# Order of the first transfers: the second chunk's gates ahead of the first part of the input weight

## The chip, the cores and the metric

The kernel runs on one core of a Trainium2 chip. The metric is device time in microseconds of one execution, lower is better. Five engines work side by side, each through its own instructions in the order in which they were written: TensorE (PE, with its weight loads as PEld), VectorE (DVE), ScalarE (ACT), GpSimd (POOL) and SyncE (SP), which here issues nearly all transfers. An instruction that waits holds up everything behind it on its engine.

## The reference

Two layers follow each other. The first is a gated linear attention over batch 4, 8 heads, 768 steps, head size 48; the second a gated feed-forward of width 384 to 1024 to 384.

```python
f = 1 / (1 + exp(-f_logit))
for t in range(S):
    state = f[:, :, t, :, None] * state + k[:, :, t] x v[:, :, t]    # outer product per head
    y[:, :, t] = q[:, :, t] @ state
x = heads of y side by side                                          # [4, 768, 384]
h = relu(x @ w_in)                                                   # w_in  [384, 1024], float64
conv = conv_w[0] * h[t-1] + conv_w[1] * h[t] + conv_w[2] * h[t+1]    # conv_w [3, 1024], float64
out = (h * sigmoid(conv)) @ w_out                                    # w_out [1024, 384], float64
```

q, k, v and f_logit are float32; the weights arrive as float64 and are made single precision on the chip.

## The kernel before, in words

**Tiling.** Time is cut into 24 chunks of 128 steps (6 for each of 4 batches, `steps`, line 106). Within a chunk the recurrence is done by matrix products: the gates' logarithms are summed over time, their exponentials scale q and k, a masked score matrix `pa`/`am` gives the part inside the chunk, a state `st` carries the rest. The result `xT` (split in a high and a low half) feeds the hidden products `ph` with w_in, then come relu, the convolution and the gate in `g`, and the output products `po` with w_out.

**Order.** All work is written as small generators, one per stage and chunk or per weight part. `ORDER` (lines 26 to 79), a string written out by hand, names at each place the generator that makes its next step: `for e in ORDER.split(): next(todo[e], None)` (line 573). The schedule is manual, so each engine gets its instructions in just this order. `F0`, `F1`, ... load the gates of chunk 0, 1, ...; `x` is exp and ln of the gates on ACT (two steps); `G` their sum over time on PE for the first six chunks; `p` the two exponentials `fi` and `fd` on ACT; `L`, `M`, `V` load k, q and v; `K` and `Q` scale k and q on DVE; `a` the scores. `I0.0` loads rows 0 to 127 and columns 0 to 511 of w_in, and the steps `J0.0` make it single precision; `c` loads and turns conv_w.

**The loads.** `load_f` and `load_w_in` each issue one transfer on SP:

```python
def load_w_in(kt, i):                                                     # line 214
    nc.sync.dma_start(raw_in(kt, i), w_in[kt * P:(kt + 1) * P, i * WC:(i + 1) * WC].bitcast(I32))
def load_f(n):                                                            # line 255
    w = FW if n < PN else NP * P
    nc.sync.dma_start(fbs[n // GC][:, n % GC]...[:, :w], chunk(f_in, *steps[n])[:, :w])
```

A gates' transfer of the first six chunks has 128 rows of 400 float32 (200 KB), the weight part 128 rows of 512 float64 (512 KB). The buffers of both are allocated before the first transfer and are not shared.

**What follows on the loads.** The first steps on ACT are, in this order, exp and ln of chunk 0 (lines 268, 271), exp of chunk 1 (268), `fi` of chunk 0 (305), ln of chunk 1 (271), `fd` of chunk 0 (307), then the third step of `J0.0` (183). `fi` and `fd` of chunk 0 read `pl`, the sum over time of chunk 0's gates (sixteen matmuls, line 292). DVE scales k of chunk 0 by `fi` (line 317) and then q by `fd` (line 324). Making a weight single (`single`, lines 173 to 189) takes six steps over three engines:

```python
nc.gpsimd.tensor_scalar(mf, hf, F64_TOP, -F64_TOP, ALU.min, ALU.max)                  # 179
nc.gpsimd.tensor_scalar(sf, mf, 0.0, 1.0, ALU.mult, ALU.mult)                          # 181
nc.scalar.activation(mf, mf, AF.Copy, scale=2.0 ** -112)                               # 183
nc.scalar.activation(lw, lw.bitcast(U32), AF.Copy, scale=2.0 ** -29)                   # 185
nc.vector.scalar_tensor_tensor(m, m, 3, s, ALU.logical_shift_left, ALU.bitwise_or)     # 187
nc.vector.tensor_tensor(w.bitcast(I32), m, lw, ALU.add)                                # 189
```

Its tiles are named `mswi` and `wi` for w_in, `mswo` and `wo` for w_out, `mscw` and `c` for conv_w. Line 386 brings the state to the next chunk on POOL (`st`), and line 398 makes the products `py`, the last of which read `st`.

Of the kernel before, what the change touches and what calls it, by code (L numbers as in the profile page):

```python
# [23 lines left out]
TS = 24  # L24
ON_POOL = ""
ORDER = """
F0 I0.0 F1 x0 x0 c L0 M0 G0 x1 I1.0 F2 J0.0 p0 x1 p0 G1 J0.0 J0.0 c J0.0 K0 p1 L1 Q0 L2 J0.0 M1 x2 c F3 V0 a0 k0 J0.0
I2.0 c p1 x2 G2 H0.0 K1 c a0 x3 J1.0 J1.0 t0 Q1 I2.1 a1 y0 J1.0 k0 y0 J1.0 c V1 H0.0 J1.0 F7 c c J1.0 x3 a1 G3 J2.0 M2
M4 p2 J2.0 p2 H1.0 F4 y0 F5 J2.0 K2 s0 J2.1 y0 J2.0 x7 J2.0 y1 J2.1 t1 s0 p3 c L3 x7 t2 Q2 k1 k1 J2.0 I0.1 x4 G7 L4 J0.1
x5 V2 M3 K3 x4 y1 H1.0 J0.1 k2 a2 k2 a2 h0.2 x5 I1.1 O3 s1 y1 s1 F6 p3 J2.1 s1 J2.1 J2.1 H2.0 y1 Q3 J0.1 G4 J2.1 J1.1 G5  # L30
# [697 lines left out]
```

## Time and profile before

| what | us |
|---|---|
| three runs | 307.47, 304.69, 305.09 |
| their median | 305.09 |
| the profiled execution, its own time | 305.0 |
| its span from first to last instruction | 303.3 |

The profiled execution thus has 1.7 us around its span, and lies 0.09 us under the median. Times in the rows count from the span's start. A row of the timeline gives the start, the duration, engine, line, operation, tiles (out<-in), shape and count, and in brackets how long the engine sat idle before and what ended it. SP's rows are the issuing of transfers, not the moving of their data.

### The profile page before, as it was taken

What the parts mean: (1) busy time and instruction counts of PE and PEld (TensorE: products, weight loads), DVE (VectorE), ACT (ScalarE), POOL (GpSimd) and SP (SyncE); (2) the same over time, 40 slices, a digit from 0 to 9 for tenths busy, and PEclk for the clock granted to TensorE, in tenths of its full rate; (3) what the DMA queues carried; (4) which work ended last, traced back from release to release, by engine and by line L of the source; (5) the groups of instructions that cost most, each with busy time, mean ns of one, the idle gap of its engine ahead of it and who ended that gap; (6) DMA issues with size and microseconds to landing.
All of it is one profiled execution on the core that took longest, in us unless ns stands there. A gap on an engine that the chain in (4) does not pass through costs nothing.

```text
span 303.3 us, 8894 instructions
## 1 busy us (share of the span) xinstructions
PE 294.2 (97%) x3747; PEld 273.5 (90%) x3747; DVE 251.3 (83%) x380; ACT 220.5 (73%) x422; POOL 85.3 (28%) x107
## 2 busy tenths in 40 slices
PE   7799989999999999999999999999999999999994
PEld 5678878988999999999998999999999999999994
DVE  4999999999999999977999999946893976479520
ACT  4999979989967996767976995665756544676521
POOL 5475894344503140300323410230305010000000
PEclk9999999999999999999999999999999999999999
DMA  7999951194025411627315130602012000000211
GB/s 230 396 385 391 403 191 39 56 333 135 2 72 161 101 59 61 220 72 224 102 37 166 64 124 2 195 2 84 3 30 89 2 28 26 28 1 2 79 54 55
DMA packets 19374, 35.67 MB, mean 118 GB/s; under 512 B 2156, under 2 KB 9092, under 8 KB 19332
## 3 DMA queue, kind: packets, MB, share of 16 engines
q1 hardware_dynamic: 19044, 34.69, 33.8%
q8 instruction: 30, 0.49, 0.7%
q10 hardware_dynamic: 288, 0.39, 0.4%
q14 instruction: 12, 0.10, 0.1%
HBM read 30.35 MB, written 4.72 MB: 116 GB/s over the span
## 4 chain that ended last, share of the span: by engine, by line
PE 75%; DVE 7%; POOL 3%; issue 1%; ACT 1%; POOLq 0%
PE po L507 31%; PE ph L454 28%; PE py L398 8%; PE pa L351 3%; PE ptk L330 2%; DVE g L466 2%; PE pk L376 2%; DVE g L464 2%; DVE g L475 1%; POOL st L386 1%; PE pa L345 1%; DVE am L358 1%; PE pk L371 1%; POOL q L324 1%; DVE gl L495 1%
## 5 line engine op out<-in xcount | busy, mean ns | idle before, releaser
L454 PE MATMUL ph<-xT,wih 128*128 128x384 f32 x384 | 99.6, 340 | 0.0
L454 PEld LDWEIGHTS ph<-xT,wih 128*128 128x128 f32 x384 | 68.3, 188 | 1.0 <-issue 0.2
L507 PE MATMUL po<-woh,gh 128*128 128x384 f32 x192 | 64.7, 337 | 0.0
L454 PE MATMUL ph<-xT,wil 128*128 128x384 f32 x192 | 64.3, 335 | 0.0
L507 PE MATMUL po<-wol,gh 128*128 128x384 f32 x192 | 64.2, 334 | 0.0
L507 PE MATMUL po<-woh,gl 128*128 128x384 f32 x192 | 64.2, 334 | 0.0
L464 DVE SCALAR_TENSOR_TENSOR g<-hb,cw,g 128x384 f32<-128x384 f32 (+1 forms) x64 | 42.2, 667 | 13.0 <-ACT g L462 12.9
L466 DVE SCALAR_TENSOR_TENSOR g<-hb,cw,g 128x384 f32<-128x384 f32 (+1 forms) x64 | 40.5, 649 | 0.7
L457 ACT ACTIVATE hb<-ph 128x384 f32<-128x384 f32 x64 | 30.7, 487 | 11.4 <-PE ph L454 10.8
L495 DVE TENSOR_TENSOR gl<-g,gh 128x1024 fp32r<-128x1024 f32 (+4 forms) x34 | 30.4, 908 | 9.6 <-ACT gh L493 9.6
L462 ACT ACTIVATE g<-hb,cw 128x384 f32<-128x384 f32 (+1 forms) x64 | 38.0, 614 | 0.3
L507 PEld LDWEIGHTS po<-woh,gh 128*128 128x128 f32 x192 | 36.0, 188 | 0.5 <-issue 0.2
L324 POOL TENSOR_TENSOR q<-q,fd 128x512 f32<-128x512 f32 x19 | 26.9, 1419 | 33.0 <-ACT fd L307 24.3
L507 PEld LDWEIGHTS po<-wol,gh 128*128 128x128 f32 x192 | 36.0, 188 | 0.0
L507 PEld LDWEIGHTS po<-woh,gl 128*128 128x128 f32 x192 | 36.0, 188 | 0.0
L454 PEld LDWEIGHTS ph<-xT,wil 128*128 128x128 f32 x192 | 36.0, 188 | 0.0
L493 ACT CAST gh<-g 128x1024 fp32r<-128x1024 f32 (+4 forms) x34 | 26.4, 800 | 12.7 <-PE po L507 8.8
L386 POOL TENSOR_TENSOR st<-st,ft_all 128x256 f32<-128x256 f32 x16 | 20.8, 1301 | 51.7 <-DVE st L384 51.7
L475 DVE SCALAR_TENSOR_TENSOR g<-g,hb 128x768 f32<-128x768 f32 (+1 forms) x32 | 30.1, 952 | 3.7 <-ACT g L473 3.7
L512 ACT COPY ob<-po 128x384 f32<-128x384 f32 x24 | 11.3, 474 | 29.7 <-PE po L507 27.1
L473 ACT ACTIVATE g<-g 128x768 f32<-128x768 f32 (+1 forms) x32 | 26.7, 846 | 3.9 <-DVE g L466 3.8
L312 POOL COPY ft_all<-fd 128x4 f32<-128x4 f32 x24 | 12.7, 537 | 56.5 <-ACT fd L307 56.5
(92 smaller groups left out, 453.9 us busy)
## 6 DMA issues: line engine op xcount, KB each, us to landing
k<-in_k_dram SPq DMA_DIRECT2D x24, 256.0 KB, 4.4
q<-in_q_dram SPq DMA_DIRECT2D x24, 256.0 KB, 4.3
v<-in_v_dram SPq DMA_DIRECT2D x24, 224.0 KB, 4.3
fb<-in_f_logit_dram SPq DMA_DIRECT2D x18, 256.0 KB, 4.3
out_dram<-ob SPq DMA_DIRECT2D x22, 192.0 KB, 1.9
wis<-in_moe_w_in_dram SPq DMA_DIRECT2D x6, 512.0 KB, 6.0
wos<-in_moe_w_out_dram SPq DMA_DIRECT2D x8, 384.0 KB, 5.6
fb<-in_f_logit_dram SPq DMA_DIRECT2D x6, 200.0 KB, 4.9
```

Of the source, the lines that this page charges most:

```text
L324: (nc.vector if n < QV else nc.gpsimd).tensor_tensor(raw["q", n], raw["q", n], fds[n][1], ALU.mult)
L398: nc.tensor.matmul(py[G * p:G * p + G, t, :], lhs, rhs, start=start, stop=stop)
L454: nc.tensor.matmul(ph, w, xts[b, hf][:, t, xl, :], start=(k == 0), stop=(k == 3 * KT - 1))
L457: nc.scalar.activation(hb[:, 2:HS + 2], ph, AF.Relu, scale=0.5)
L462: nc.scalar.activation(cv, hb[:, 1:n + 1], AF.Copy, scale=cw[:, 1, f:f + 1])
L464: nc.vector.scalar_tensor_tensor(cv, hb[:, 2:n + 2], cw[:, 2, f:f + 1], cv, ALU.mult, ALU.add)
L466: nc.vector.scalar_tensor_tensor(cv, hb[:, 0:n], cw[:, 0, f:f + 1], cv, ALU.mult, ALU.add)
L473: nc.scalar.activation(cv, cv, AF.Tanh)
L475: nc.vector.scalar_tensor_tensor(cv, cv, 1.0, h_b[:, fp:fp + 2, 1:n + 1], ALU.add, ALU.mult)
L493: nc.scalar.copy(hi, g[:, f:f + k])
L495: nc.vector.tensor_tensor(lo, g[:, f:f + k], hi.bitcast(F32), ALU.subtract)
L507: nc.tensor.matmul(po, g[:, f, :], w, start=(i == 0), stop=(i == 3 * NF - 1))
```

## The change

Two neighbouring words of `ORDER`, the second and the third, change places. SP issues the gates of chunk 1 second and the first part of w_in third; every other transfer keeps its place, and no engine other than SP gets its instructions in another order.

```diff
 ORDER = """
-F0 I0.0 F1 x0 x0 c L0 M0 G0 x1 I1.0 F2 J0.0 p0 x1 p0 G1 J0.0 J0.0 c J0.0 K0 p1 L1 Q0 L2 J0.0 M1 x2 c F3 V0 a0 k0 J0.0
+F0 F1 I0.0 x0 x0 c L0 M0 G0 x1 I1.0 F2 J0.0 p0 x1 p0 G1 J0.0 J0.0 c J0.0 K0 p1 L1 Q0 L2 J0.0 M1 x2 c F3 V0 a0 k0 J0.0
 I2.0 c p1 x2 G2 H0.0 K1 c a0 x3 J1.0 J1.0 t0 Q1 I2.1 a1 y0 J1.0 k0 y0 J1.0 c V1 H0.0 J1.0 F7 c c J1.0 x3 a1 G3 J2.0 M2
```

## Rows read from the trace of the kernel before

**Rows 1.** The page: busy shares, then granted clock and DMA share in 40 slices.

```profile
PE 294.2 (97%) x3747; PEld 273.5 (90%) x3747; DVE 251.3 (83%) x380; ACT 220.5 (73%) x422; POOL 85.3 (28%) x107
...
PEclk9999999999999999999999999999999999999999
DMA  7999951194025411627315130602012000000211
```

**Rows 2.** The chain that ended last, in order of time: start, us, what.

```profile
39.11 4.25 POOL st L386
...
43.41 0.80 PE py L398 x24
```

**Rows 3.** Timeline of DVE, three stretches between 7 and 40 us.

```profile
7.60 0.69 DVE L317 TENSOR_TENSOR k<-k,fi 128x512 f32<-128x512 f32 x1 [2.17 <-ACT fi L305]
8.51 0.69 DVE L324 TENSOR_TENSOR q<-q,fd 128x512 f32<-128x512 f32 x1 [0.22 <-ACT fd L307]
...
35.95 1.03 DVE L195 TENSOR_TENSOR wil<-wi,wih 128x512 fp32r<-128x512 f32 x1
...
39.13 0.54 DVE L187 SCALAR_TENSOR_TENSOR mswo<-mswo 128x384 int32<-128x384 int32 x1
```

**Rows 4.** Waits of DVE from 8 to 46 us: who waited for what, us in total, times, longest.

```profile
DVE k L317 <- ACT fi L305: 2.2, 1, 2.2
DVE q L324 <- ACT fd L307: 0.2, 1, 0.2
```

**Rows 5.** Timeline of SP, the first 7 us.

```profile
1.36 0.42 SPq L215 DMA_DIRECT2D wis<-in_moe_w_in_dram  x1
1.82 0.43 SPq L259 DMA_DIRECT2D fb<-in_f_logit_dram  x1
...
4.60 1.48 SPq L276 DMA_DIRECT2D k<-in_k_dram  x2
```

**Rows 6.** Timeline of ACT from 3 to 13 us.

```profile
3.43 0.54 ACT L268 ACTIVATE fb<-fb 128x400 f32<-128x400 f32 x1 [1.26 <-DMA fb<-in_f_logit_dram]
4.00 0.54 ACT L271 ACTIVATE fb<-fb 128x400 f32<-128x400 f32 x1
6.48 0.54 ACT L268 ACTIVATE fb<-fb 128x400 f32<-128x400 f32 x1 [1.95 <-DMA fb<-in_f_logit_dram]
6.97 0.60 ACT L305 ACTIVATE fi<-pl 128x512 f32<-128x512 f32 x1
...
8.36 0.63 ACT L183 ACTIVATE mswi<-mswi 128x512 f32<-128x512 f32 x1
...
9.93 0.53 ACT L268 ACTIVATE fb<-fb 128x400 f32<-128x400 f32 x1
10.36 0.29 ACT L183 ACTIVATE mscw<-mscw 24x128 f32<-24x128 f32 x1
```

**Rows 7.** Timeline of POOL, three stretches between 5 and 44 us.

```profile
5.82 0.65 POOL L179 TENSOR_SCALAR mswi<-wis 128x512 f32<-128x512 f32 x1 [2.61 <-DMA wis<-in_moe_w_in_dram]
6.56 0.62 POOL L181 TENSOR_SCALAR mswi<-mswi 128x512 f32<-128x512 f32 x1
7.26 0.28 POOL L179 TENSOR_SCALAR mscw<-cws 24x128 f32<-24x128 f32 x1
7.63 0.82 POOL L181 TENSOR_SCALAR mscw<-mscw 24x128 f32<-24x128 f32 x1
...
35.55 0.88 POOL L179 TENSOR_SCALAR mswo<-wos 128x384 f32<-128x384 f32 x1
...
39.08 4.27 POOL L386 TENSOR_TENSOR st<-st,ft_all 128x256 f32<-128x256 f32 x1
```

**Rows 8.** Waits of SP from 0 to 40 us: who waited for what, us, times, longest.

```profile
SPq L276 <- DMA wis<-in_moe_w_in_dram: 0.7, 2, 0.5
```

**Rows 9.** Timeline of PE from 4 to 9 us.

```profile
4.95 1.98 PE L292 MATMUL pl<-tri,fb 128*64 128x128 f32 x16
```

**Rows 10.** Waits of PE over the whole span, one of five.

```profile
PE py L398 <- POOL st L386: 1.1, 1, 1.1
```

## Prediction

> **What bounds the kernel now.** I read the page first. PE is busy in 97% of the span, at the full granted clock in every slice; DMA is full in slices 1 to 5, that is from about 2 to 40 us, and far from full after that [rows 1]. So there is a head of some 43 us, in which inputs and weights arrive and are prepared, and then a long stretch that PE fills. Whatever changes in the order of the first transfers can only act through the head. Next I read the chain that ended last: it enters the PE stretch at 43.41, released by POOL's state product of 39.11 to 43.36 [rows 2]. To see what sets 43.4 us, I read the waits of DVE: from 8 to 46 us it has only two, one of 2.2 us that ends at 7.60 and one of 0.2 us that ends at 8.51 [rows 3, 4]. From then on DVE works without a pause until the end of the head, so a shift of DVE at 9 us is still there at 43, and from there goes into PE and the end. Last I read the timelines of SP, ACT, POOL and PE for the first 11 us, to see who stands before DVE's two waits.
>
> **The issues.** SP issued the weight at 1.36 and the gates of chunk 1 at 1.82, each for about 0.43 us, none waiting [rows 5]. They change places: gates at 1.36, weight at about 1.80. Nothing is added. They land one behind the other: POOL, which waits for the weight, starts at 5.82, and ACT, which waits for the gates, at 6.48, 0.66 later [rows 6, 7]. With the bytes ahead unchanged, the later of the two should land when the later one landed before: the weight at about 6.4. For the gates I take 3.43 (ACT's start on chunk 0's gates [rows 6]) plus 0.66, so 4.1; at worst 200/512 of the 2.39 us that the weight took from 3.43 to 5.82, so 4.4. The transfers behind (conv_w, k, q, the next weight) see the same sum of bytes ahead. One thing does move on SP: of the two k's issued from 4.60, the stretch is 1.48 us in place of twice some 0.43 [rows 5], so the second waited, and the waits of SP put that to the landing of a weight, 0.5 us at the longest [rows 8]. Now the gates hold that place and land first, and this k is issued up to 0.5 us sooner; it queues behind DMAs that are full anyway, so I count nothing.
>
> **What goes: ACT's wait of 1.95 us before exp of chunk 1.** ACT is free from 4.54 (4.00 + 0.54), so exp can run from then, two microseconds sooner. But behind it stands `fi` of chunk 0, which reads `pl`, and PE works on `pl` until 4.95 + 1.98 = 6.93 [rows 9]. `fi` starts at 6.97, 0.49 after exp; elsewhere ACT starts the next instruction 0.43 after the same exp (9.93 to 10.36) [rows 6]. So `fi` was waiting for PE already, and the wait that goes is replaced by another one that ends at the same time. Ends: nothing, or at most 0.06 (0.49 less 0.43). I take 0. The ln of chunk 1 stands behind `fi` and stays too.
>
> **What comes later: the weight, by about 0.64 us** (POOL's start at 5.82 becomes 6.46, about where ACT's start at 6.48 was). POOL's first step then runs 6.46 to 7.11, and the second, which followed at a distance of 0.74, from 7.20 to 7.82 [rows 7]. ACT wants it at 8.36 [rows 6]: 0.5 us of cover are left. Conv_w's two steps on POOL, which ended at 8.45, come some 0.6 later and are wanted on ACT at 10.36: covered too. For data alone the cost is nothing. It would cost only if the weight landed more than 1.18 us later than before (8.36 less 7.18, the end of POOL's second step).
>
> **What collides: POOL with DVE.** The second step moves from 6.56 to 7.18, when DVE was idle, to 7.20 to 7.82, and at 7.60 DVE starts on k of chunk 0 [rows 3, 7]. Such pairs hold each other up in this trace. Conv_w's second step, 24 rows of 128, took 0.82 where its first took 0.28: it began at 7.63, under DVE's k product, and ended 0.16 after that one (8.29). In the other direction, POOL's step at 35.55 stretched DVE's product at 35.95 to 1.03, where products of the same width take 0.69 [rows 3, 7]. So DVE's k product waits for POOL until 7.82 (0.22 late), ending at 8.51; just there q starts, which had an idle 0.22 in front. This swallows it: cost 0.0 to 0.1. Then conv_w's two steps (0.28 each) meet k and q instead of one of them meeting k alone; each can hold DVE once, at most 0.28, and DVE has no idle time left behind q. Upper end: 0.22 + 0.28 + 0.28 less the 0.22 idle, 0.56. Lower end: 0, if POOL does all the waiting, for it has 0.5 us and more to give. There is no row of this very pattern; the nearest is 35.55, where POOL slipped in once and cost DVE 0.34. I take a third of the upper end, 0.2, as one of the two conv_w steps finds DVE free at some point.
>
> The Trainium skill, page "SBUF — State Buffer", section "Who interferes with whom", says that a VectorE instruction with two SBUF inputs and a GpSimd instruction that reads SBUF exclude each other, and that the one that starts second blocks until the first is done. By it the k product at 7.60 loses to POOL's step and the q product loses nothing as long as conv_w's steps start behind it, which would make the sum 0.0 to 0.1 in place of 0.2. The trace agrees at 7.63 and 35.55; at 39.08 it doesn't, for there POOL started 0.05 before DVE and still took 4.27 us [rows 3, 7].
>
> **The sum.** 0.0 from ACT, 0.0 from SP and the DMAs, +0.2 from POOL against DVE, carried by DVE to 43 us and by PE to the end: 305.0 + 0.2 = 305.2 us against the profiled execution, 0.1 above the median of 305.09. That is far under 1% (3 us), about what a measurement of this kernel can tell from no change; the runs shown differ by 2.8 us among themselves.
>
> **Rivals.**
>
> (a) Faster, the wait was worth its length: 1.95 us off ACT and the end, 303.05. For it: it is ACT's longest wait in the stretch shown, and ACT's instructions stand close behind it [rows 6]. Against: `fi` can't start before `pl` is done at 6.93, and DVE waits for `fi`.
>
> (b) Faster, a race near the end of the head turns. POOL's state product took 4.27 us at 39.08, since DVE began a long run of products at 39.13 [rows 3, 7]; PE waited 1.1 us for it [rows 10]. If the shift lets POOL in first, PE gains up to this 1.1: 305.2 - 1.1 = 304.1. Against: what stands before both there follows DVE, so both are shifted alike and the distance of 0.05 stays.
>
> (c) Slower: the weight lands so late that POOL's second step starts under DVE's k product and has to wait for its end. The place is 7.6 us; it decides from a landing some 0.4 us later than I take (second step starting at 7.60 in place of 7.20). POOL then starts it at 8.29 and ends at 8.91, ACT's step of 8.36 waits until 8.95, 0.59 late, and POOL holds q on DVE from 8.51 to 8.91, 0.40 late. Both engines go on without a pause: 305.0 + 0.6 = 305.6. For it: the weight is the largest of the early transfers. Against: the sum of bytes ahead.
>
> (d) The swap does nothing at all, as the gates land together with the weight: 305.0.
>
> **How the numbers follow.** The forecast has 0.75: its own range is 304.9 (all gained, nothing paid: 305.0 less 0.06) to 305.6 (305.0 + 0.56). (a) has 0.04, since the row of `pl` speaks plainly against it; (b) 0.07; (c) 0.11; (d) 0.03. The range goes down to (b)'s 304.1, rounded to 304.0, and up beyond (c) to 306.5: a run of the kernel before has stood 2.4 us above its median, and a race as in (b) lost elsewhere would cost about the same 1.1 (305.2 + 1.1 = 306.3). None of the cases reaches 1% in either direction (302.0 or 308.1). The chances of that are what the scatter of runs and races that I don't see leave: 0.02 faster, 0.03 slower, 0.95 within 1%.
>
> **What would show it.** Right: ACT's exp of chunk 1 starts between 4.5 and 5 with no wait for a DMA; `fi` still starts at 6.9 to 7.0, now after a wait of about 2 us for PE; POOL's first wait, for the weight, ends near 6.45, about 0.65 later; ACT's step of line 183 still starts at 8.3 to 8.5; DVE's k product takes 0.8 to 1.0 in place of 0.69; the state product of POOL near 39 still takes about 4 us, and PE enters its stretch at 43.3 to 44.0. Wrong: `fi` starting well before 6.9 (rival a), a state product under 1.5 us near 39 (b), line 183 waiting for POOL (c), gates landing after 5.5 (d), or a change of more than 1 us that none of these rows accounts for.

## The result and the profile after

| | before | after |
|---|---|---|
| median of 16 runs each, us | 304.96 | 307.26 |
| lowest and highest | 304.03, 308.26 | 305.72, 308.29 |
| profiled execution, its span | 305.0, 303.3 | 306.96, 305.2 |

The ratio is 1.0064 with an interval of [1.0040, 1.0089]: slower, by 0.64% or about 2 us. That is under the 1% that I had named, but it is real, and it lies outside the range given (304.0 to 306.5). The two profiled executions differ by 1.96 us and their spans by 1.9, so they show a loss of that size.

The page of after, granted clock and DMA share in 40 slices, as in [rows 1]:

```profile
PEclk9789999999999999999999999999999999999999
DMA  6999981185023422527305230602003000000211
```

Two things are new. The granted clock is below full in the second and third slice, and the DMAs move a little less at the start and more later. The timeline of after, PE, ACT, DVE and POOL from 4.7 us, answers to [rows 3, 6, 7, 9]:

```profile
4.76 0.52 ACT L268 ACTIVATE fb<-fb 128x400 f32<-128x400 f32 x1
...
5.00 1.09 PE L292 MATMUL pl<-tri,fb 128*64 128x128 f32 x16 [0.29 <-ACT fb L271]
...
6.13 0.60 ACT L305 ACTIVATE fi<-pl 128x512 f32<-128x512 f32 x1 [0.85 <-PE pl L292]
...
7.34 0.68 POOL L179 TENSOR_SCALAR mswi<-wis 128x512 f32<-128x512 f32 x1 [4.14 <-DMA wis<-in_moe_w_in_dram]
...
8.06 0.69 DVE L317 TENSOR_TENSOR k<-k,fi 128x512 f32<-128x512 f32 x1 [2.63 <-DMA k<-in_k_dram]
8.10 1.13 POOL L181 TENSOR_SCALAR mswi<-mswi 128x512 f32<-128x512 f32 x1
...
8.68 1.08 DVE L324 TENSOR_TENSOR q<-q,fd 128x512 f32<-128x512 f32 x1
9.26 0.63 ACT L183 ACTIVATE mswi<-mswi 128x512 f32<-128x512 f32 x1 [1.62 <-POOL mswi L181]
...
9.82 1.16 PE L345 MATMUL pa<-q,k 48*128 48x128 f32 x16 [1.52 <-DVE q L324]
...
11.36 0.69 DVE L317 TENSOR_TENSOR k<-k,fi 128x512 f32<-128x512 f32 x1
```

Read from the top. Exp of chunk 1 starts at 4.76 without a wait, as the swap wanted. `fi` then waits for PE, and goes at 6.13, even earlier than the 6.97 of before, since PE's sum `pl` took 1.09 here and 1.98 there [rows 9]. But POOL gets the weight at 7.34, where it had it at 5.82 [rows 7], and DVE, which had waited for `fi` until 7.60 [rows 3], now waits until 8.06 for k of chunk 0 itself. POOL's second step starts 0.04 behind it and shares the stretch with both products of DVE: 1.13 for POOL, 1.08 for q in place of 0.69. ACT's step of line 183 waits 1.62 for POOL and starts at 9.26, 0.90 later than in [rows 6]. k of chunk 1 on DVE comes at 11.36.

Next the windows, first of before, then of after. Columns: stretch, its length, busy time (and count) of PE, PEld, DVE, ACT and POOL, granted clock, DMA share, GB/s.

```profile
3.00:4.00 1.00, 1.00 (x4) 0.73 (x4) 0.79 (x2) 0.54 (x2) 0.21 (x3) 1.00 1.10 315
4.00:5.00 1.00, 1.00 (x5) 0.35 (x3) 0.94 (x5) 0.53 (x1) 0.00 (x0) 1.00 0.88 260
5.00:6.00 1.00, 1.00 (x11) 1.00 (x12) 0.35 (x2) 0.00 (x0) 0.18 (x1) 1.00 1.02 302
6.00:7.00 1.00, 0.92 (x10) 0.52 (x6) 0.00 (x0) 0.52 (x2) 0.92 (x2) 1.00 1.18 403
7.00:8.00 1.00, 0.00 (x0) 0.00 (x0) 0.40 (x1) 1.00 (x4) 0.84 (x3) 1.00 0.91 326
8.00:10.00 2.00, 1.84 (x28) 1.60 (x30) 1.65 (x4) 2.00 (x5) 0.45 (x1) 1.00 1.01 381
10.00:15.00 5.00, 3.93 (x72) 3.21 (x72) 5.00 (x9) 4.94 (x13) 2.58 (x4) 1.00 1.04 409
15.00:20.00 5.00, 4.93 (x132) 3.59 (x122) 5.00 (x10) 4.97 (x11) 4.66 (x6) 1.00 1.06 395
```

```profile
3.00:4.00 1.00, 1.00 (x4) 0.73 (x4) 0.79 (x2) 0.25 (x1) 0.20 (x3) 1.00 0.82 286
4.00:5.00 1.00, 0.71 (x3) 0.32 (x2) 0.94 (x5) 0.97 (x3) 0.00 (x0) 1.00 0.91 218
5.00:6.00 1.00, 1.00 (x16) 0.85 (x16) 0.35 (x2) 0.28 (x1) 0.00 (x0) 1.00 0.74 164
6.00:7.00 1.00, 0.10 (x2) 0.00 (x0) 0.00 (x0) 0.87 (x2) 0.00 (x0) 1.00 0.81 288
7.00:8.00 1.00, 0.79 (x14) 0.80 (x16) 0.00 (x0) 0.64 (x2) 0.66 (x1) 1.00 1.06 395
8.00:10.00 2.00, 0.48 (x8) 0.24 (x6) 1.78 (x3) 0.74 (x2) 1.76 (x4) 1.00 1.00 354
10.00:15.00 5.00, 4.36 (x40) 3.51 (x41) 4.87 (x8) 5.00 (x13) 3.06 (x4) 0.61 1.05 414
15.00:20.00 5.00, 5.00 (x95) 4.23 (x93) 3.62 (x7) 3.04 (x8) 3.52 (x6) 0.71 0.94 292
```

The clock's column reads 1.00 also where the trace has no record of the clock: the records begin at 7.28 us in before and at 4.28 in after. What holds ahead of them is seen from PE's own rows: the 1.98 of `pl` in before is the length that such a sum has at half the clock further down (1.97), so that sum, too, ran at the lower clock.

From 3 to 6 us the DMAs moved 315 + 260 + 302 = 877 KB before and 286 + 218 + 164 = 668 KB after: the stream is 209 KB short, half a microsecond at the 400 GB/s of later stretches. And from 10 to 20 us PE has a granted clock of 0.61 and 0.71 in place of 1.00: for part of it PE ran at 1.2 instead of 2.4 GHz. Between 6 and 10 us PE had been busy for 0.92 + 0.00 + 1.84 = 2.76 us before, and for 0.10 + 0.79 + 0.48 = 1.37 after.

The chain that ended last, in order of time, shows how the two come together. It answers to [rows 2].

```profile
2.79 5.17 DMA k<-in_k_dram
...
8.06 0.58 DVE k L317
...
8.68 1.09 DVE q L324
...
9.80 0.68 ACT wis L185
...
12.52 1.97 PE pl L292 x16
...
26.32 8.17 DMA v<-in_v_dram
34.50 0.14 issue
...
46.14 4.01 PE ph L454 x22
```

The chain begins with a transfer, k of chunk 0, goes over DVE and ACT, and meets PE's sum `pl` of the third chunk at 12.52, which takes 1.97 at the lower clock. In before the same sum ran from 11.61 to 12.70. Its end thus moves by 1.79: 0.91 since it starts later, 0.88 from the clock. Behind it stands SP: the rows of SP's waits and of its timeline for the transfer that waits for this `pl`, first of before, then of after.

```profile
SPq L259 <- PE pl L292: 2.5, 1, 2.5
12.79 0.33 SPq L259 DMA_DIRECT2D fb<-in_f_logit_dram  x1
```

```profile
SPq L259 <- PE pl L292: 3.7, 1, 3.7
14.59 0.33 SPq L259 DMA_DIRECT2D fb<-in_f_logit_dram  x1
```

These gates can only be fetched when PE has read the older ones in the same buffer, and SP issues in order. So this transfer goes 1.80 us later, and by SP's timeline the next ones go 1.8 to 2.8 us later. That is how a delay at 12 us reaches 34.50 (the end of v on the chain) and the entry into the long PE stretch: 46.14, against 44.21 (43.41 + 0.80 [rows 2]). These 1.93 us are the whole difference of the two spans.

### The profile page after: what moved, and what is told of

The parts are those of the page before. It is cut to its first block, busy times and chain, and to the rows that moved or that the text cites. A ratio compares the mean times of both kernels' runs of the same rounds, so it can differ in the third digit from the quotient of the medians.

```text
span 305.2 us, 8894 instructions
## 1 busy us (share of the span) xinstructions
PE 295.7 (97%) x3747; PEld 275.1 (90%) x3747; DVE 251.6 (82%) x380; ACT 220.2 (72%) x422; POOL 83.2 (27%) x107
## 4 chain that ended last, share of the span: by engine, by line
PE 80%; DVE 8%; DMA 6%; ACT 2%; issue 1%; SPq 1%; DVEq 0%
PE po L507 30%; PE ph L454 29%; PE py L398 10%; PE pa L351 3%; DMA v<-in_v_dram 3%; PE ptk L330 2%; PE pa L345 2%; DMA q<-in_q_dram 2%; DMA k<-in_k_dram 2%; DVE g L466 2%; DVE g L464 2%; PE pk L376 1%; DVE g L475 1%; PE pk L371 1%; PE pl L292 1%
## 5 line engine op out<-in xcount | busy, mean ns | idle before, releaser
L457 ACT ACTIVATE hb<-ph 128x384 f32<-128x384 f32 x64 | 30.7, 486 | 11.4 <-PE ph L454 10.8
L512 ACT COPY ob<-po 128x384 f32<-128x384 f32 x24 | 11.3, 475 | 29.5 <-PE po L507 26.9
L386 POOL TENSOR_TENSOR st<-st,ft_all 128x256 f32<-128x256 f32 x16 | 17.5, 1091 | 51.4 <-DVE st L384 51.4
```

Of the source, the lines that this page charges most:

```text
L457: nc.scalar.activation(hb[:, 2:HS + 2], ph, AF.Relu, scale=0.5)
```

## The experiments

The theory from these rows had two parts. Lateness: the weight lands 1.5 us later (issued at 1.36 and 4.4 to its landing before, at 1.82 and 5.4 after), k of chunk 0 0.8 us (both issued at 2.8, then 4.4 and 5.2), and DVE, ACT and SP carry that on. Clock: as PE has less to do before 11 us, its clock falls for a while and costs more on top. For every execution of the experiments the granted clock is on record, and I speak of a "fall" where its mean over the span is at most 0.994. The mean starts with the first record, so a clock that rises late doesn't show in it.

**1. PE kept busy.** Eight products of zeros, four behind each of the first two sums; and for comparison four in the kernel before, and that kernel unchanged.

```diff
-F0 F1 I0.0 x0 x0 c L0 M0 G0 x1 I1.0 F2 J0.0 p0 x1 p0 G1 J0.0 ...
+F0 F1 I0.0 x0 x0 c L0 M0 G0 w0 x1 I1.0 F2 J0.0 p0 x1 p0 G1 w1 J0.0 ...
+    def warm(n):
+        for _ in range(n):
+            nc.tensor.matmul(pa[:, 0, 0, :], zr[:, :P], zr[:, :P], start=True, stop=True)
+        yield
```

a_fill (after, w0 and w1): 

> The changed kernel, with eight matmuls of zeros on PE, four behind the sums of chunk 0 and four behind those of chunk 1, where PE stands idle for 1.1 and 1.5 us in the changed kernel; nothing else waits for them. Theory (the granted clock's fall between 11 and 18 us costs the greater part): no fall, mean granted clock 1.0 in all executions, and 305.7 to 306.2 us, the level of the four executions of the changed kernel with a clock near 1.0; some 1 us above the kernel before stays. Rival (the late weight and the late k cost everything, the clock's fall is hidden behind DVE and the DMAs): the clock stays up but the time stays at 307.0 to 307.5.

b_fill (before, w0 alone): 

> The kernel before, with four matmuls of zeros on PE behind the sums of chunk 0, nothing else: the control. Theory (clock): the kernel before loses its clock in only some of its executions, those of 307 us and more; with the matmuls these go, and the median stays at 304.6 to 305.0. Rival: the matmuls do something of their own to the order of the head, and the median moves by more than 0.5 us either way.

b_again: 

> The kernel before once more, to see the granted clock of each execution beside its time. Theory (clock): its executions fall in two groups, clock 1.0 at 304 to 305.1 us and clock near 0.99 at 306.5 to 308. Rival: no relation between its clock and its time.

Measured: a_fill 305.57 (12 runs), ratio to before 1.0026 [0.9997, 1.0055]; two falls in 12. b_fill 304.26 (13 runs), 0.9974 [0.9947, 1.0002]; no fall. b_again 304.45 (12 runs), 0.9992 [0.9960, 1.0025]; four falls. A repeat of b_fill on another chip:

b_fill_again: 

> The kernel before with the four matmuls of zeros once more: 304.0 to 304.6 and no execution with a fallen clock, as in the 13 before; against the kernel before a ratio of 0.996 to 0.999, which would make it the fastest form seen here.

304.62 (12 runs), 0.9981 [0.9955, 1.0006], no fall: none in 25 executions of the two, but no speed beyond the kernel before that could be told apart from it. The windows of a_fill:

```profile
8.00:10.00 2.00, 1.78 (x20) 1.43 (x18) 1.80 (x3) 0.76 (x2) 1.75 (x4) 1.00 1.01 364
10.00:15.00 5.00, 3.72 (x52) 3.01 (x50) 4.87 (x8) 5.00 (x12) 3.08 (x4) 1.00 1.04 411
```

With the filler PE is busy for 1.78 of the two microseconds, the clock stays at 1.00 in the profiled execution, and the median is 1.7 us under that of after. Not all of the 1.7 need count for the swap: with the filler the kernel before is lower too, by 0.57 and 0.27 us (against 304.83 and 304.89 in the same comparisons), though not clear of the noise. A rest stays: the weight, k and the product of DVE on k of chunk 1 (11.37) are as late as in after, and a_fill stands 1.3 and 0.95 us above the two runs of before with the filler (305.57 less 304.26 and 304.62). Of the 2.3 us between the orders about half thus goes with the falls, as far as pairs with eight and with four products can be compared.

**2. The weight, or k?** The weight's transfer moved on to the sixth place, so that k and q land early and the weight late.

```diff
-F0 F1 I0.0 x0 x0 c L0 M0 G0 x1 ...
+F0 F1 x0 x0 c L0 M0 I0.0 G0 x1 ...
```

> The changed kernel with the first part of w_in moved on from the third to the sixth place, behind conv_w, k and q of chunk 0. Theory A (what costs beside the clock is the weight's late landing, by way of POOL): the weight lands some 1.3 us later still (k and q together take 1.33 us), POOL, and ACT behind it, another 1.3 us late: 308 to 309. Theory B (what costs is the late landing of k, on which DVE waits): k lands near 5.0, DVE starts at fi, near 6.8, and the time comes down to 306 or less.

Measured: 307.90 (7 runs), 1.0092 [1.0060, 1.0124], a fall in all seven. From its timeline:

```profile
7.29 0.69 DVE L317 TENSOR_TENSOR k<-k,fi 128x512 f32<-128x512 f32 x1 [1.87 <-ACT fi L305]
...
9.00 0.65 POOL L179 TENSOR_SCALAR mswi<-wis 128x512 f32<-128x512 f32 x1 [5.81 <-DMA wis<-in_moe_w_in_dram]
...
10.39 0.63 ACT L183 ACTIVATE mswi<-mswi 128x512 f32<-128x512 f32 x1 [2.22 <-POOL mswi L181]
...
12.48 0.68 DVE L317 TENSOR_TENSOR k<-k,fi 128x512 f32<-128x512 f32 x1
```

The first product of DVE is 0.77 earlier than in after and the kernel is no faster, so an early k of chunk 0 does not help by itself; what it is worth with the weight in its old place was not tried. The late weight holds ACT at line 183, ACT holds DVE, and k of chunk 1 comes 1.1 us later than in after, all by the written order. The median is only some 0.6 us above that of after, less than 1.1. Neither expectation came true: 308 to 309 for one, 306 or less for the other.

**3. The gates by another queue.** Chunk 1's gates are issued by ACT, so that SP's next ones move up. With the filler too.

```diff
-        nc.sync.dma_start(fbs[n // GC]...
+        (nc.scalar if n == 1 else nc.sync).dma_start(fbs[n // GC]...
```

f1_act: 

> The changed kernel, but the gates of chunk 1 are issued by ACT, on its own queue, ahead of ACT's first exp; on SP the weight thus stands second again, as in the kernel before. The gates still come early, the weight is not queued behind them. Theory (it is the weight's place in the queue that costs, and by it also the granted clock): the weight lands at 5.7 to 6.1, POOL takes it up by 6.2, PE's score product of chunk 0 starts by 9.3, and the time is 304.3 to 305.2, that of the kernel before, with a fall of the clock in no more than half of the executions. Rival (early gates alone unsettle PE, since the sums of chunk 1 come early and leave a longer gap behind them): the clock falls in most executions and the time is 306.5 or more.

f1_act_fill: 

> The same with the eight matmuls of zeros on PE, so that the clock plays no part. Theory: 304.0 to 304.6, level with the kernel before with its four matmuls (304.26), some 1.2 us below the changed kernel with the eight matmuls (305.57). Rival: near 305.5, as there.

Measured: 305.84 (12 runs, 304.57 to 309.36), 1.0062 [1.0034, 1.0091]; with filler 306.04 (12 runs), 1.0054 [1.0021, 1.0087]. Falls: 3 in 12, and none in 12 with filler. The weight came about as the theory had it, but the times fit neither theory nor rival in either run. Two queues now share the DMAs from the start, so that both gates land at about 4.8, which moves PE's first sum to 5.96 in the profiled execution of f1_act. Here it is, and below it the same sum and the first filler in f1_act_fill:

```profile
5.96 1.09 PE L292 MATMUL pl<-tri,fb 128*64 128x128 f32 x16 [1.33 <-ACT fb L271]
```

```profile
6.11 1.98 PE L292 MATMUL pl<-tri,fb 128*64 128x128 f32 x16 [1.10 <-ACT fb L271]
...
8.02 2.08 PE L533 MATMUL pa<-st 128*128 128x128 f32 x8
```

In the second, the first record of the clock at full is at 10.36: the sum and the filler ran at the lower one, and `fi` went at 8.12, against 7.09 in f1_act. That execution took 307.31, without a fall. The best executions of f1_act (304.57, 304.73, 304.87) are level with the kernel before (304.25), others far above, some of them at a mean clock of 1.00 (307.72, 308.33, 308.47). So there is lateness that no fall explains. From 3 to 6 us the DMAs of the two runs move 1044 and 1059 KB, more than in any other, and POOL has the weight at 6.22 and 6.28: full DMAs at the start did not bring the time back.

**4. The weight's later steps moved back in the written order.** If ACT and DVE only lose time standing before the weight, let the chunk's own work go first.

```diff
-... G1 w1 J0.0 J0.0 c J0.0 K0 p1 L1 Q0 L2 J0.0 M1 x2 c F3 V0 a0 k0 J0.0
-I2.0 c p1 x2 G2 H0.0 K1 c a0 x3 ...
+... G1 w1 J0.0 c K0 p1 L1 Q0 L2 M1 x2 J0.0 J0.0 c F3 V0 a0 k0
+I2.0 c p1 x2 G2 K1 J0.0 J0.0 H0.0 c a0 x3 ...
```

a_use_late_fill: 

> The changed kernel with the eight matmuls of zeros, and with the third to sixth step on the first weight part (ACT, ACT, DVE, DVE) written some places later: on ACT behind fi of chunk 1 and exp of chunk 2, on DVE behind k of chunk 1, so that chunk 1 no longer stands behind the late weight. To be read against the next run, which has the same order of steps with the transfers as before. Theory (the rest of the loss comes by the weight's own chain over POOL, ACT and DVE): it loses no more than 0.5 us against the next run, where the pair without the moved steps stood 1.3 apart (305.57 and 304.26); what stays is k of chunk 0, which landed 0.45 after DVE could have used it. Rival (all transfers behind the weight are late, and DVE and PE wait for these just the same): the distance stays at 1.0 to 1.4 us.

b_use_late_fill: 

> The kernel before with four matmuls of zeros and with the same steps on the first weight part written later: the partner of the run above. Both theories: within 1 us of 304.3, as the steps that move have the same length; only the distance to the run above tells the theories apart.

Measured: 309.33 (6 runs), 1.0142 [1.0104, 1.0179], and 306.81 (6 runs), 1.0087 [1.0058, 1.0117]. The distance of 2.5 us fits neither expectation. The new order alone costs more than 2 us (306.81 against 304.26 and 304.62) and brings falls back, in 5 of 6 and 3 of 6 executions. Inconclusive.

**5. POOL's collision with DVE.** ACT makes the sign's tile of line 181 for this one weight part (0 times `mf`, in which the sign is lost), so POOL has one step less.

```diff
-        nc.gpsimd.tensor_scalar(sf, mf, 0.0, 1.0, ALU.mult, ALU.mult)
+        if nm == "wi0_0":
+            nc.scalar.activation(sf, mf, AF.Copy, scale=0.0)
+        else:
+            nc.gpsimd.tensor_scalar(sf, mf, 0.0, 1.0, ALU.mult, ALU.mult)
```

a_step2_act_fill: 

> The changed kernel with the eight matmuls of zeros (305.57 us), and with the second step on the first weight part (line 181) on ACT, which stands idle there for 1.4 us, and no longer on POOL. Theory (what is left of the loss when the clock stays up comes from POOL's second step, late by the weight, which shares its time with the k and q products on DVE and keeps ACT waiting): DVE's q product takes 0.69 in place of 1.05, ACT's step of line 183 starts near 8.7 in place of 9.24, DVE's k product of chunk 1 near 10.8 in place of 11.37, and the time is 304.7 to 305.2. Rival (the loss sits in the later transfers, which are as late as before): these starts move, but the time stays at 305.4 to 305.8.

a_step2_act: 

> The same without the matmuls of zeros, to be read against the changed kernel (307.26). Theory: PE's score product of chunk 0 starts 0.5 us sooner, PE's idle stretch is shorter and the clock falls in fewer than 12 of 16 executions; 305.5 to 306.7. Rival: the falls stay as frequent, 306.8 or more.

Measured: with filler 306.00 (12 runs), 1.0017 [0.9981, 1.0053], 3 falls; without 306.84 (12 runs), 1.0043 [1.0007, 1.0078], 8 falls. With filler this can't be told from a_fill. Its profiled execution shows one reason: the q product takes 0.77 instead of 1.05, but DVE's k of chunk 1 stands at 11.38 all the same, now for its own transfer.

```profile
8.95 0.77 DVE L327 TENSOR_TENSOR q<-q,fd 128x512 f32<-128x512 f32 x1
...
11.38 1.05 DVE L320 TENSOR_TENSOR k<-k,fi 128x512 f32<-128x512 f32 x1 [0.24 <-DMA k<-in_k_dram]
```

The collision is there, and in this execution taking it away gained nothing, since the transfer of k itself was late by as much. That does not hold for every execution: in the profiled one without filler POOL had the weight at 6.67, k of chunk 1 went at 10.97, and it took 304.80. What the collision costs stays open.

**6. The weight in two transfers** of 256 columns each.

```diff
-        nc.sync.dma_start(raw_in(kt, i), w_in[kt * P:(kt + 1) * P, i * WC:(i + 1) * WC].bitcast(I32))
+        m = 2 if (kt, i) == (0, 0) else 1
+        for j in range(m):
+            n = WC // m
+            c = i * WC + j * n
+            nc.sync.dma_start(raw_in(kt, i)[:, 2 * j * n:2 * (j + 1) * n], w_in[kt * P:(kt + 1) * P, c:c + n].bitcast(I32))
```

> The changed kernel with the first weight part sent as two transfers of 256 columns each (2 KB rows) in the same place, one behind the other. Theory (the weight's own slow transfer, some 3 us behind the gates where later parts of equal size take 1.3, is what is late; in smaller rows it spreads more evenly over the DMAs): both halves have landed by 6.7, POOL starts by 6.8, and the time falls to 306.3 or less. Rival (its rows' size is not the cause; the first bytes of this matrix are slow in any form): the second half lands at 7.0 to 7.5 and the time stays at 307 to 308, as one more issue on SP comes on top.

Measured: 306.88 (12 runs), 1.0047 [1.0016, 1.0078], 9 falls; POOL gets the second half at 7.46. Smaller pieces don't bring the weight in sooner.

**7. Early gates without their bytes.** Is it the bytes of the gates that make the weight late, and is it the early gates in themselves that cost anything? Chunk 1's transfer is cut to 16 of 400 columns, in both orders; DVE writes a constant into the rest of the tile (in the second pair POOL, since DVE came to it only at 5.45).

```diff
         w = FW if n < PN else NP * P
+        if n == 1:
+            nc.vector.memset(fbs[0][:, 1].rearrange("p n t -> p (n t)")[:, 16:FW], 4.0)
+            w = 16
```

a_f1_thin: 

> The order of after, but the transfer of chunk 1's gates carries only 16 of their 400 columns (the rest of that tile is set to one constant on DVE at the start, so the gates of that chunk are not the real ones). Chunk 1's gates are thus there at least as early as in after, while the weight, k and q have only some 8 KB in front of them in place of 200 KB. Theory 'late stream' (all of the loss comes from the weight, k and q landing about 0.8 us later, and the falls of the clock follow from PE's work starting later): weight lands 5.0 to 6.2, k product of chunk 1 on DVE at 10.0 to 10.7, and the time is that of b_f1_thin within 0.5 us, with as many executions that show a fall. Rival 'early gates' (it is ACT and PE being moved by the early gates that costs): 1.5 to 2.3 us slower than b_f1_thin. Third case 'slow start' (a transfer of short rows ahead of the weight is what makes the weight slow, whatever its bytes): weight lands later than in b_f1_thin by 0.4 or more.

b_f1_thin: 

> The order of before with the same 16 of 400 columns of chunk 1's gates behind the weight. Both theories: 303.5 to 305 us, weight at 5.7 to 5.9, k of chunk 0 about 0.5 us earlier than before's 7.15; the number that counts is the distance of a_f1_thin to this one: within 0.5 us ('late stream') or 1.5 to 2.3 ('early gates').

a_again: 

> The changed kernel itself beside the two. 'Late stream' and 'early gates' both: 306 to 307.5, in two of three executions a mean granted clock of 0.994 or less. If it comes out within 0.5 us of the kernel before here, the loss depends on the chip or the hour, and the distance of the first result is no property of the order.

a_f1_thin2: 

> a_f1_thin once more, with the constant written by POOL, which is idle there, in place of DVE, which had written it so late (5.45 to 5.83 us) that chunk 1's exp on ACT was no earlier than 5.86; the gates of chunk 1 are again not the real ones. Now exp of chunk 1 starts at about 4.6 as in after, and the weight should again land near 7.1, k near 7.8. 'Late stream': distance to b_f1_thin2 as in the first pair (0.3 where no fall of the clock shows, 0.75 over all), falls in about 5 of 12 executions. Rival 'early gates': distance 1.5 to 2.3 over all, falls in 8 or more of 12, PE idle for longer before 8 us than in a_f1_thin.

b_f1_thin2: 

> Partner of a_f1_thin2 in the order of before, constant on POOL. Exp of chunk 1 at about 5.3 (its 8 KB land behind the weight), weight at 5.0 to 5.9; 304 to 305 us, at most 2 of 12 executions with a fall.

| | median, runs | ratio to before | falls |
|---|---|---|---|
| a_f1_thin | 305.42, 12 | 1.0027 [1.0003, 1.0051] | 5 |
| b_f1_thin | 304.67, 12 | 0.9985 [0.9962, 1.0008] | 1 |
| a_again | 306.78, 12 | 1.0056 [1.0025, 1.0088] | 11 |
| a_f1_thin2 | 305.31, 12 | 1.0020 [0.9992, 1.0047] | 6 |
| b_f1_thin2 | 304.69, 12 | 0.9998 [0.9977, 1.0019] | 3 |

The rows of the second pair, chunk 1's exp and the weight on POOL, first a_f1_thin2, then b_f1_thin2 (ACT's and DVE's line numbers are 3 higher here):

```profile
4.47 0.52 ACT L271 ACTIVATE fb<-fb 128x400 f32<-128x400 f32 x1
...
7.09 0.66 POOL L179 TENSOR_SCALAR mswi<-wis 128x512 f32<-128x512 f32 x1 [3.53 <-DMA wis<-in_moe_w_in_dram]
```

```profile
5.33 0.65 POOL L179 TENSOR_SCALAR mswi<-wis 128x512 f32<-128x512 f32 x1 [1.77 <-DMA wis<-in_moe_w_in_dram]
5.52 0.54 ACT L271 ACTIVATE fb<-fb 128x400 f32<-128x400 f32 x1 [0.97 <-DMA fb<-in_f_logit_dram]
```

With 8 KB of chunk 1's gates ahead in place of 200 KB the weight still comes at 7.09, 1.76 later than in the other order. The bytes of these gates are not what makes the weight late: the third case of the expectation. The pairs differ by 0.75 and 0.62 us, just above the "within 0.5" of the theory of the late stream and far under the 1.5 to 2.3 of the early gates, with the early exp (4.47) as without it (5.86 in the first pair). And a_again repeats the loss on its chip: 2.0 us (306.78 less the 304.79 of the kernel before there). With a weight as late as in after, the kernels without these bytes thus lose only a third of that.

**8. Place or gates.** The kernel before with conv_w's small transfer second, the weight third, the gates fourth.

```diff
-F0 I0.0 F1 x0 x0 c L0 M0 G0 ...
+F0 c I0.0 F1 x0 x0 L0 M0 G0 ...
```

> The order of before, but conv_w's transfer (24 KB in 24 rows) goes second, the weight third, chunk 1's gates fourth. 'Third place' (a weight that is issued third runs slowly whatever short transfer stands in second place, because too little is under way behind the first one): weight lands at 6.5 to 7.3, and 1500 to 1640 KB are landed by 8 us. Rival 'gates' (only rows of gates ahead slow it, 128 of them, whatever their length): weight at 5.2 to 6.1, 1700 KB or more by 8 us. The time: chunk 1's gates land last of the three, so exp, fi and k come late by 0.5 to 1 us in the first case: 305 to 307; in the second 304.5 to 306.

Measured: 307.10 (12 runs), 1.0057 [1.0027, 1.0087], 10 falls. From its windows and its timeline:

```profile
3.00:4.00 1.00, 1.00 (x4) 0.73 (x4) 0.79 (x2) 0.58 (x2) 0.20 (x3) 1.00 0.76 151
4.00:5.00 1.00, 1.00 (x5) 0.39 (x5) 0.94 (x5) 0.49 (x1) 0.00 (x0) 1.00 0.90 246
5.00:6.00 1.00, 1.00 (x16) 0.76 (x16) 0.36 (x2) 0.00 (x0) 0.00 (x0) 1.00 0.85 297
```

```profile
6.50 0.63 POOL L179 TENSOR_SCALAR mswi<-wis 128x512 f32<-128x512 f32 x1 [3.30 <-DMA wis<-in_moe_w_in_dram]
```

24 KB ahead of the weight make it 0.68 later than the 5.82 of before; at 400 GB/s they are worth 0.06. The landing, at 6.4, lies between the two expectations, the 1744 KB moved by 8 us fit the rival, and the time is above both ranges. From 3 to 6 us the DMAs moved 151 + 246 + 297 = 694 KB. Over the profiled executions of all kernels that load these by SP alone, the same sum goes with the weight's place: 798 to 932 KB in the seven with it second (before 877, b_fill_again 798, b_f1_thin2 932), 641 to 753 in the ten with it third (after 668, a_again 753, a_weight_halves 641). It isn't a small transfer in second place as such, though: a_weight_fifth, with conv_w third, k fourth and the weight sixth, has 826. The kernel b_c_second also has falls of the clock with no early gates at all: chunk 1's exp is later here (6.92) than in before (6.48).

## Why the prediction was wrong

**What held.** Exp of chunk 1 went at 4.76 without a wait, `fi` waited for PE's `pl`, and the removed wait bought nothing: rival (a), 303.05, is out. Its sign, `fi` well before 6.9, did come (6.13), but not from the removed wait: PE's sum was shorter, and in a_again, where it took 1.90, `fi` went at 6.89. The early `fi` bought nothing either, as DVE then waited for k. POOL's second step did run under DVE's k product and held up q.

**The step that failed first** is the one on the issues: "With the bytes ahead unchanged, the later of the two should land when the later one landed before: the weight at about 6.4". POOL had it at 7.34. The argument needs DMAs that are full while the weight moves. I had read that from slices of 7.6 us, and of these the first shows 7 tenths [rows 1]. The windows of one microsecond show what it hides: shares of 0.82, 0.91 and 0.74 from 3 to 6 us in after. In these kernels the order went with how much the DMAs moved, and not only with what came first; by what means was not found. For the same reason "the transfers behind see the same sum of bytes ahead" failed; k landed 0.8 us late (at 7.96 on the chain, behind the 7.60 at which DVE took it before), and the sum had no term for that. Nor was SP's 0.0 right: behind its second k it waited 1.2 us for the weight, and issued the next q at 7.28 in place of 6.48.

**The collision** was sized at +0.2, with a weight at 6.4; on DVE it took 0.39 (q 1.08 in place of 0.69; k, which was to take 0.8 to 1.0, kept its 0.69). The prediction's own limit for the data, a weight 1.18 us later, was passed too (7.34 less 5.82 is 1.52): without any collision POOL's second step would have ended at 8.72 (8.10 + 0.62), 0.36 behind the 8.36 at which ACT took it before. The collision stretched the step by another 0.51. Rival (c) had the right mechanism: it named a landing 0.4 later than I took as its point, and the landing came 0.9 later. It put line 183 at 0.59 late and its own price at 0.6; line 183 was 0.90 late and the loss was 2.3 between the medians. Experiment 5 shows an execution in which the collision is gone and chunk 1's k is just as late.

**The path** failed as well. DVE was to carry the delay to 43 us without a pause. In after DVE waits four times more from 9 to 46 us, 2.1 us in all, and the chain goes from PE's late sum over SP to the transfers of q and v.

**The term that was missing** is the clock. I read "full granted clock in every slice" [rows 1] as a property of the kernel. It is one of that execution, and even there not of the first 7.28 us, of which there is no record. Of 158 executions of the kernel before whose clock is on record, 53 show a fall (median 306.08, the others 304.36). Of 28 of the changed kernel, 23 do (307.25, the other five 305.80). So a third has become four fifths. Nor are all falls alike: a mean clock of 0.989 or less, as in the profiled execution of after, costs more than one of 0.991 to 0.994, as in that of a_again. Medians and numbers of executions by depth:

| mean clock | before | after |
|---|---|---|
| above 0.994 | 304.36 (105) | 305.80 (5) |
| 0.991 to 0.994 | 305.53 (38) | 306.67 (7) |
| 0.989 or less | 307.34 (15) | 307.42 (16) |

So the loss has two parts that don't simply add up. Deep falls went from a tenth of the executions to more than half, and a deep fall costs 3.0 us in the kernel before itself. Without a fall, or with a shallow one, the changed kernel is some 1.1 to 1.4 us later, by few executions; with a deep one the two stand level. Why the lateness doesn't show there is not known.

**What hangs together how.** Shown: the filler takes away most falls and about half of the loss (experiment 1); an early k of chunk 0 does not help by itself (2); the bytes of chunk 1's gates are not what makes the weight late (7). Seen together, but not shown as cause: falls are more frequent where the weight comes late, with early gates or without (2, 7, 8). Not shown: one single carrier of the remaining lateness. In the profiled execution of a_step2_act_fill the weight's steps and chunk 1's own transfers reach DVE at about 11.4 us together, so that taking away one left the other. In the profiled executions without a fall, the work order of the kernel kept, DVE's start on k of chunk 1 goes with the time, though not in step: 10.4 to 11.1 us with 303.8 to 305.2 us, 11.3 to 11.6 us with 305.1 to 306.5 us, the kernel before with filler (11.30, 306.54) among them; f1_act_fill, with its late clock, has 11.94 and 307.3. The thin pairs, whose weight is 1.8 to 2.1 us later, differ there by only 0.5 to 0.6 us, and by 0.4 us in the time without falls (305.01, 13 executions, against 304.61, 20), so the weight's landing alone doesn't set the price. That too stays open in its size.

**Rival (b)** came true on the side: the state product near 39 us took 4.27 in before, and in after none on POOL between 30 and 46 us takes over 0.7. In b_again, which is the kernel before itself, the one at 38.91 took 0.60. Such a race turns from one execution to the next, and says nothing on a change.

## What to carry to other kernels

A sum of bytes says when a transfer lands only where the DMAs are full, and the first microseconds must be looked at in windows of one microsecond before that is assumed; a large transfer issued early may be what keeps them full (798 to 932 KB against 641 to 753 here, for reasons not found). Where an engine's gap is filled or opened near the start, ask in how many executions the granted clock falls, not whether it fell in the one that was profiled, and compare medians of executions without a fall and with falls of like depth. A wait that vanishes from one engine is worth nothing if the next instruction there has a second wait that ends at the same time, and the place that it gave up may belong to a transfer on which three engines stand.

## What the runs showed of the hardware that I had not expected

- The first part of the weight is slow wherever it stands. By issue and time to landing it lands some 2.4 us behind the transfer ahead of it in second place (3.4 to 5.8 in before) and 3.0 in third (4.2 to 7.2 in after), where 512 KB at the 400 GB/s of later stretches are 1.3 us. What leaves the gaps was not found; fewer bytes ahead, fewer rows ahead or smaller pieces don't close them. A second queue does (1044 and 1059 KB in experiment 3), without bringing the weight in sooner than 6.22.
- PE's first sum `pl` took 1.98 us in before and 1.09 in after, started 0.05 apart. The records of the granted clock show it at full from 7.28 in the one and from 4.28 in the other. a_again, the same kernel as after, took 1.90. Over all profiled executions the first record at full lies between 4.10 and 10.36 us, and for the one order of after at 4.28 and 6.63. So the order of the kernel alone does not set when the clock first rises.
- A stretch at the lower clock comes with more than slower matmuls. In after, ACT and DVE are busy for 3.04 and 3.62 of the five microseconds from 15, where they had 4.97 and 5.00, and the DMAs move 292 GB/s in place of 395, as SP stands behind PE's sum; part of that sum's delay is its late start.
- POOL's step that starts under a product of DVE gets in between it and the next one, although that follows without a pause: k 0.69 as ever, POOL 1.13, q 1.08 (8.06 to 9.76).
